# Block-sparse attention and a maxout layer: values as column tiles of TensorE, run in one session with the scores

## The chip, the cores and the metric

The kernel runs on one core of a Trainium2 chip. What counts is the device time of one execution in microseconds, as the median of several runs. A core has five engines that run side by side, each through its own list of instructions in a fixed order: TensorE (PE; its weight loads are shown as PEld), VectorE (DVE), ScalarE (ACT), GpSimd (POOL) and SyncE (SP), which here only issues DMAs. They wait for one another through semaphores. Matmuls write to PSUM, eight banks of 512 f32 per partition; everything else lies in SBUF.

## What is computed

Four batches of eight heads, 768 positions, 64 dimensions a head. A position attends to its neighbours within 15 places and to 24 summaries of blocks of 32 (the maximum of the keys, the mean of the values); the heads' outputs side by side go through a maxout layer.

```
k_sum = k.reshape(B, H, nb, block, D).max(axis=3)
v_sum = v.reshape(B, H, nb, block, D).mean(axis=3)
scores_l = scale * q @ k.T          # masked to |i - j| < 16
scores_s = scale * q @ k_sum.T + log(block)
a = softmax(concatenate([scores_l, scores_s]))
x = a @ concatenate([v, v_sum])     # heads side by side: (3072, 512)
h1 = x @ w1; h2 = x @ w2            # (3072, 1024)
out = maximum(h1, h2) @ w_out       # (3072, 512)
```

## The kernel before

Positions are cut into 12 tiles of 64 queries per head. For a tile, 128 keys stand in the partitions: 64 in its middle, the 32 rows of block summaries (24 used), and 32 of the next tile (`kx`, columns 96 apart). So one matmul per head and tile, with `kx` as weights and 64 queries moving, gives all scores of the tile, keys in the partitions. It contracts over the 64 dimensions of one head. Two heads lie in the two halves of the partitions, so the matmuls of a pair of heads use the upper and the lower 64 rows of the array. Four tiles make a group (`grp` 0 to 2), and a head pair (`hp` 0 to 3) with a group is a *unit*.

`scores` (L473) takes two units in one go: 16 matmuls of 64 rows into two PSUM banks, one bank per head of the pair. In batch 0 the mask is first put into the banks by TensorE (L504: four full matmuls with the identity as weights and `hide`, 0 or -29952, as what moves). In later batches the mask is multiplied in afterwards by VectorE (L545, or twice L549 for the last group, where the window wraps around). Between the two, ScalarE takes the exponential of each bank (L537) into a tile `pb` of four pieces of 192 columns: 64 weights, 64 zeros, 64 weights. The zeros are set once (L246, 12 tiles).

`values` (L558) works on one unit: eight matmuls, each with 128 columns of `pb` as weights and 65 columns of `vx` (values and a one) moving. The zeros let two tiles be accumulated into one output: the first matmul takes weights and zeros, the second zeros and weights, so that one tile's queries come out in partitions 0 to 63 and the other's in 64 to 127. The 65th column is the softmax's denominator: VectorE takes its reciprocal (L580) and multiplies (L582) into `xs`, one unit at a time. `xs` is then turned by TensorE (L594 in batch 0, whole; `turn_x`, L608, in later batches, by half rows) and copied to `xt`.

The maxout layer needs `xt`: `hidden` blocks (L708, eight matmuls of 256 columns with the difference w2 - w1, `wd`), a relu on ScalarE or VectorE (L397, L399), and `out` blocks (L722 on x with w1 w_out, made once by L692; L729 on the relu with w_out), four matmuls of 512 columns each. That is by max(h1, h2) = h1 + relu(h2 - h1).

Every step is recorded by `op` with engine, inputs and outputs (`Plan`, L109); nothing is scheduled when the kernel is built. The string `ORDER` (L20 to L72) lists all 777 steps in one order, with the engine of each (P, A, D, G, S) and the buffer that it takes; per engine, this is the order of the instructions. The costs given to `op` are not used in the run. PSUM's eight banks are one ring that all steps share; so are eight landing buffers `land` for loads. SP's list holds all loads, the stores of the output, and some copies within SBUF that lay out the values (`vx<-vb`, `vx<-vx`).

`first_attention` (L778) does batch 0: k and q are turned whole (L425), scores, then values. `later_attention` (L749) does batches 1 to 3 a head pair at a time: k and q are turned by half rows (`turn_halves`, L440) within the same step as the scores of the pair before (`with_turn`), and a turn of `xs` within another (`with_x`), so that steps which use half the rows stand together. `load_w12` and `split_w12` (L642, L653) load w1 and w2 and make `wd` and `w1b`; `fixed_parts` (L233) makes zeros and masks.

Of the kernel before, what the change touches and what calls it, by code (L numbers as in the profile page):

```python
# [20 lines left out]
    "D11 S23:0,0 D17:0 S27:1 D2 D6 G18 D3 G16:0 D13 S49:2,0 D14 S47:3,0 S48:0 A79:0 G43:0,0,0 G19 P81:0 "  # L21
    "G20 S24:0 G21 A83:2,0 S25:4 D84:0 G28:0,0 D9 S52:5,0 D86 A39 P44:1 G41 S51:0 G88:1 A106:2 S53:6 G42 "
    "A45 P90:2 D89:3 D0 A92:3,0 P91:3 G80:0 A96:0 P108:4 D93:1 G34:0,0 A110:0,0 P82:5 D95 S50:0 D40 A87:1 "
    "D94 D85 D38 S63:7 P97:6,7 D46 S73:1 D26:0 A98:7 D112 A99:2 P35:0 D29 D30 A116:1 P103:1,2 D111:0 "
    "G115:3 S76:3 A36 P118:3 D113 A105:9 D37 S54:0 P117:4 A104:10 G56:0 D123:2 A60:1 P100:5,6 D32 A107:2 "
    "G31 P57:7 S182:4,0 D119:2,0 A102:5 P61:0 D10 P109:2 D120:1 G33 A101:6 P133:1 A114:3 D70:0 P136:3 "
    "S181:0 D121 A58:1,0 P71:4 D137:0 D122 D138:0 P124:6,5 D134:1 D135 D62:0 G74:0 P149:2 A126:2 P152:3 "
    "D150:2 S64:5 D72:0 A125:7 G75:0 D153:0 D151:1 A66:1 P127:7,1 D154 P144:0 G77:0 P141:5 A128:5 P548:4 "
    "D145:1 D142:2 S183:2,0 A129:6 P551:6 A78:0 S184:0 P67:2 P130:3,7 G59:0 D68:0 S185:1,0 P545:1 D146:2 "
    "D143 P157:2 P139:0 P546 G253:0 A140:0 S191:3 A131:2 P549 G22:0 D547:0 A254:1 P147:5 D55:0 P552 "  # L30
    "A132:7 S189:4 P255:0 G65:0 S186:0 A550:0 D553:0 P165:3 P554:7 A256:3,0 D148 S188:0,0 D166:0 D158:1 "
    "P559:4 D167:3 D159:4 A262:3 G261:2 P168:6 D257:0 P176:5 P155:3 G273:0 P555 A156:1 D177:2 D178:5 "
    "P561:2 D8 G198:1,0,0,0 A556:0 D69:0 S187:0 P160:3 P570:5 A562:0 D258 D161:0 A560 D169:1 P557:7 D259 "
    "D162 A260:0 D170 G192:0,0 P173:2 P563:4 D558 P263:3,6,0 A564 S206:6,0 P565:7 D264:0,0 A271:9 S205:0 "
    "P571 D174:2 D265:1 G190:0 S208:2,0 P566 D175 P572 A274:1 D268:1 A269:10 P179:4 P163:6 D196 P567 "
    "A573:0 D164 P199:2 G308:2 A568:1 P171:0 P581:1 D266 A203 D267 A201 D172:2 G309:3 A202 D200 "
    "P275:3,5,6 D270 S204 P575:0 G320:0 S195 D276:2,0 A283:4 S212:5,0 P577:2 A582:1 G197 D576 S207:0 "
    "A281:5 G321:1 P583:5 D277:0 S232:7,0 A280:2 P579:1 D193 A578 S230:3,0 P285:0,3 A580 D180 P588:6 D194 "
    "A288:6 S215:4 P584 A286:2 D282 S209:1,0 D278 P589 D279 D272 D284 P310:7,2,3 S229:0 D287 P293:1 "
    "G359:2 P599:0 D311:0,0 A318:7 G358:3 P302:2 D294:0 P585 A600:2 D295:0 D313 D303:1 P299:1 D304 P597:0 "  # L40
    "A586:2 D289 A315:3 P590 D312:1 A598 P296:2 D319 P593:5 A316:4 D300:2 D314 A591:3 P595:3 D317 A594 "
    "D297:0 G216:0,0 S592 D301:2 P322:4,0,6 D298:1 A596 S210:0 P290:5 S235:0,0 P305:1 A328:5 P601:2 "
    "D291:1 S213:6 D306:2 D292 A330:9 S569 D329 P338:3 A323:3,0 P602 D307 S587 D339:0 D331 S211:0 "
    "P332:4,5,0 A327:0 D340:5 D324:0 G371:0 P347:3 P603 A334:10 D348:1 A336:2 D325 P341:6 D349 P606:7 "
    "D335 A418:1 D337 P350:4 P607 A333:3 D342:2 D351:0 D343:4 D352 P344:3 A604:3 P353:5 D345:1 P608 D326 "
    "D354:2 G214:0 D346:3 D355 P360:6,4,0 A609:1 P356:2 G370:2 A361:0,0 S218:0,0,0 P223:5 D357 G221 "
    "A224:0 A227 G406:3 A225 D362:1 P615:7 A366:6 G246:1,0,0,0 G222 D365:1 A226 P617:2 A368:4 S228 D364 "
    "P613:3 S236:0 D363 A618:0 D5 S605 A616 P372:6,5,0 S220 A614 P611:4 G405:0 D373:2,0 S217 A380:7 "
    "P624:2 A378:5 D612 S219 P619:7 D417:2 S237:2 D374:0 P382:3,5 P625 S239:4 A383:9 D377:2 P620 A385:2 "
    "D375 D376 P631:6 D386 D384 P407:4,3,0 D369 P626 D632:1 A408:0,0 P633:5 A415:10 D627:2 P621 A413:1 "  # L50
    "D367 S628 D410 D381 P629:6 D409:1 A622:3 A634 P390:3 P651:2 D412:3 A630 P635:4 D411 D391:0 D414 "
    "P387:7 D392:0 G238:0,0 P642:5 A636 D15 D388:1 P419:6,0,3 D379 P643 D389:1 A425:4 D416 P637:1 "
    "A420:3,0 D426 P402:7 A427:6 G240:0 P396:6 P644 D397:2 A424:0 D398 P638 D403:0 A652:2 G456:0 D404:2 "
    "S241 A645:2 P399:0 S242 P393:6 D428 P653:3 G244 D400:1 S243 D394:2 D401 S231:0 P649:4 D395 A654 "
    "D421:0 S646 P429:2,7,5 A650 P435:0 G502:3 P639 A433:11 D436:0 D437:3 A431:5 P438:3 D430:0 P647:4 "
    "S234:6,0 P444:7 D432 P660:0 A648 S233:0 D12 D445:1 D439:2 P655:2 D423 S574 D446 D422 P447:5 D440:4 "
    "P661 A640:2 D434 A503:1 D448:0 P247:6 S641 D449 G455:2 P450:4 P441:7 A249 P656 A248 D245 A251 D451:1 "
    "D442:2 D452:5 P662 D443 D250 P453:3 A663:0 P457:1,5,6 D454 P657 G468:0 A458:0,0 P689:0 D467:2 A658:2 "
# [94 lines left out]
def kernel(  # L153
# [14 lines left out]
    nc = tc.nc  # L168
# [673 lines left out]
```

## Time and profile before

| | |
|---|---|
| median of 5 runs | 181.19 us (177.85 to 183.35) |
| profiled execution | 178.53 us |
| its span, first to last instruction | 176.9 us |
| granted TensorE clock | 1.000 |
| moved by DMA | 35.30 MB, mean 200 GB/s |
| instructions on DVE / ACT / POOL | 275 / 155 / 64 |

The page's slices cut the span into 40 parts of 4.4 us; each digit is the busy share in tenths. The groups name a line of the kernel, the engine, the operation, what it writes and reads, and how often; after the bar stand the busy time, the mean length of one in ns, and the idle time just before them with what ended it. In the timeline the first number is the start, the second the length of the merged stretch; matmuls overlap one another in the records (each is shown for some 190 ns or more), so what a stretch costs is read from its start to the start of the next one.

A core's transfers are 25.17 MB read from HBM and 6.29 MB written, and the copies inside SBUF. A load of k or q of a head pair is 384 KB, of half the values of a batch 768 KB, of a half of w1, w2 or w_out 1024 KB.

### The profile page before, as it was taken

The page shows a single profiled execution, that of the slowest core. Times are in us where ns is not written, and L with a number is a line of the kernel's source. Part 1 is how long each engine was busy: PE and PEld are TensorE (multiplying, and loading weights), DVE is VectorE, ACT ScalarE, POOL GpSimd, SP SyncE. Part 2 cuts the span into 40 slices and gives each one's busy share as a digit, 9 for nine tenths or more (in the row PEclk, how much of TensorE's full clock was granted, in tenths as well). Part 3 has the DMA queues.
Part 4 walks back from the last instruction along what each step waited for, and adds up shares of the span by engine and source line. Part 5 has one row for each costly group of instructions (what it writes and reads, how often), then busy time and mean ns, then how long its engine had stood idle before and what let it go on. Part 6 is the DMA issues. An engine that isn't in the chain of part 4 may idle for free.

```text
span 176.9 us, 5119 instructions
## 1 busy us (share of the span) xinstructions
PE 158.2 (89%) x2160; PEld 107.3 (61%) x2160; DVE 109.4 (62%) x275; ACT 95.0 (54%) x155; POOL 50.6 (29%) x64
## 2 busy tenths in 40 slices
PE   0165979999999999979999999799999999999992
PEld 0154756657657676657576675488556657865461
DVE  2219998399879976757978666477565445613030
ACT  3378478576367578849274661585663742140011
POOL 6490545678338413164003751100000000000000
PEclk9999999999999999999999999999999999999999
DMA  5999999999997999977999298555003102100553
GB/s 152 279 308 313 386 386 387 380 366 181 271 367 160 296 280 325 263 224 161 277 213 222 77 208 242 207 153 113 0 4 119 65 0 90 32 0 0 182 175 122
DMA packets 43767, 35.30 MB, mean 200 GB/s; under 512 B 25952, under 2 KB 37728, under 8 KB 43744
## 3 DMA queue, kind: packets, MB, share of 16 engines
q1 hardware_dynamic: 43744, 34.98, 71.5%
q8 instruction: 17, 0.28, 0.7%
q14 instruction: 6, 0.05, 0.1%
HBM read 25.17 MB, written 6.29 MB: 178 GB/s over the span
## 4 chain that ended last, share of the span: by engine, by line
PE 67%; DMA 11%; DVE 7%; SPq 4%; POOL 3%; ACT 3%; issue 3%; POOLq 0%; ACTq 0%
PE banks L708 22%; PE banks L729 19%; PE banks L722 10%; PE banks L569 4%; PE banks L692 4%; DMA out_dram<-o 4%; DMA land<-in_v_dram 4%; DMA land<-in_q_dram 3%; DVE vx L401 3%; PE banks L508 2%; PE banks L440 2%; SPq L296 2%; POOL vb L401 2%; DVE ks L458 2%; ACT o L401 1%
## 5 line engine op out<-in xcount | busy, mean ns | idle before, releaser
L708 PE MATMUL banks<-xt,wd 128*128 128x256 bf16 x384 | 46.2, 273 | 0.5 <-ACT o L401 0.5
L729 PE MATMUL banks<-wo,g 128*128 128x512 bf16 (+1 forms) x200 | 46.6, 371 | 0.0
L708 PEld LDWEIGHTS <-wd 128*128 128x128 bf16 x384 | 36.5, 98 | 7.3 <-issue 0.8
L537 ACT ACTIVATE pb<-banks,bias 128x512 bf16<-128x512 f32 x48 | 31.6, 690 | 15.1 <-PE banks L508 13.6
L397 ACT ACTIVATE g<-banks 128x512 bf16<-128x512 f32 x34 | 20.0, 601 | 22.4 <-PE banks L708 22.4
L729 PEld LDWEIGHTS <-g 128*128 128x128 bf16 x200 | 18.2, 98 | 16.8
L401 POOL CAST kqb<-land 128x768 bf16<-128x768 f32 x20 | 18.4, 920 | 25.6 <-PE banks L440 8.4
L722 PE MATMUL banks<-w1o,xt 128*128 128x512 bf16 (+1 forms) x100 | 24.0, 371 | 0.0
L401 ACT COPY o<-banks 128x512 f32<-128x512 f32 (+1 forms) x19 | 10.6, 567 | 23.9 <-PE banks L729 10.2
L458 DVE TENSOR_REDUCE ks<-kx 128x24 bf16<-128x768 bf16 x16 | 15.2, 947 | 8.1 <-ACT kx L401 8.1
L582 DVE TENSOR_TENSOR xs<-banks,inv 128x256 bf16<-128x256 f32 x48 | 19.1, 415 | 0.5
L401 POOL CAST vb<-land 128x1536 bf16<-128x1536 f32 x7 | 10.4, 1482 | 27.2 <-DMA land<-in_v_dram 25.2
L569 PEld LDWEIGHTS <-pb 128*128 128x128 bf16 x384 | 15.4, 97 | 4.3 <-ACT pb L537 0.2
L580 DVE RECIPROCAL inv<-banks 128x4 f32<-128x4 f32 x48 | 8.2, 177 | 15.9 <-PE banks L569 14.3
L569 PE MATMUL banks<-vx,pb 128*128 128x65 bf16 x384 | 17.5, 193 | 0.1
L722 PEld LDWEIGHTS <-xt 128*128 128x128 bf16 x100 | 9.1, 98 | 8.3
L401 DVE COPY o<-banks 128x512 f32<-128x512 f32 x6 | 4.1, 691 | 15.0 <-PE banks L729 15.0
L399 DVE TENSOR_SCALAR g<-banks 128x512 bf16<-128x512 f32 x14 | 9.7, 690 | 5.6 <-PE banks L708 5.6
L545 DVE TENSOR_TENSOR pb<-pb,mask 128x512 bf16<-128x512 bf16 x24 | 11.5, 485 | 0.9 <-ACT pb L537 0.7
L401 ACT CAST kqb<-land 128x768 bf16<-128x768 f32 x9 | 7.5, 833 | 7.2 <-DMA land<-in_q_dram 5.0
L425 PE MATMUL banks<-identity,kqb 128*128 128x128 bf16 x48 | 5.5, 301 | 5.9 <-ACT kqb L401 5.1
L508 PE MATMUL banks<-qx,kx 64*128 64x64 bf16 (+2 forms) x416 | 10.4, 193 | 0.2 <-ACT qx L401 0.2
(67 smaller groups left out, 170.5 us busy)
## 6 DMA issues: line engine op xcount, KB each, us to landing
land<-in_k_dram SPq DMA_DIRECT2D x16, 384.0 KB, 6.2
land<-in_v_dram SPq DMA_DIRECT2D x8, 768.0 KB, 8.9
land<-in_q_dram SPq DMA_DIRECT2D x16, 384.0 KB, 6.4
out_dram<-o SPq DMA_DIRECT2D x19, 256.0 KB, 3.3
land<-in_moe_w_dram SPq DMA_DIRECT2D x4, 1024.0 KB, 12.3
land<-in_moe_w_out_dram SPq DMA_DIRECT2D x2, 1024.0 KB, 13.7
vx<-vb SPq DMA_DIRECT2D x4, 396.0 KB, 5.2
vx<-vx SPq DMA_DIRECT2D x3, 363.0 KB, 4.3
```

Of the source, the lines that this page charges most:

```text
L397: nc.scalar.activation(out=o, in_=i, func=ACT.Relu)
L399: nc.vector.tensor_scalar_max(out=o, in0=i, scalar1=0.0)
L401: {"DVE": nc.vector.tensor_copy, "ACT": nc.scalar.copy, "POOL": nc.gpsimd.tensor_copy, "SP": nc.sync.dma_start}[e](out=o, in_=i)
L458: op("DVE", 0.95, lambda: nc.vector.tensor_reduce(out=ks.ap[:].rearrange("p (t s) -> p t s", s=2), in_=kt()[:, :, 0:64].rearrange("p t (s ...
L508: nc.tensor.matmul(**m)
L537: op("ACT", 0.7, lambda a=a, pv=pv: nc.scalar.activation(out=pv(), in_=bank(pss[a]).rearrange("p (i w q) -> p i w q", w=2, q=64), func=ACT ...
L545: nc.vector.tensor_tensor(out=pv(), in0=pv(), in1=m, op=ALU.mult)
L569: nc.tensor.matmul(out=av()[:, u, a, :], lhsT=pbs[a].ap[:, 2 * at + u, 64 * par:64 * par + 128], rhs=vx[b].ap[:, 4 * grp + 2 * u + par, 2 ...
L582: op("DVE", 0.42, lambda: nc.vector.tensor_tensor(out=x.ap[:, hp % 2], in0=av()[:, :, :, 0:D], in1=inv.ap[:].to_broadcast([128, 2, 2, D]), ...
L708: nc.tensor.matmul(out=bank(ps)[:, 256 * s:256 * s + 256], lhsT=wd[n].ap[:, c, 128 * s:128 * s + 128], rhs=x_rows(b, grp)[:, c, :], start= ...
L722: nc.tensor.matmul(out=bank(ps, hi - lo), lhsT=x_rows(b, grp)[:, c, sl], rhs=w1o[c].ap[:, lo:hi], start=(c == 0), stop=False)
L729: nc.tensor.matmul(out=bank(ps, hi - lo), lhsT=g.ap[:, f, sl], rhs=wo[f // 2].ap[:, f % 2, lo:hi], start=False, stop=(f == FC - 1))
```

## The change

*Values.* `pb` has no zeros any more: six tiles of two heads by 512 columns. A values matmul takes 64 columns of `pb` as weights instead of 128 and writes 64 partitions, the upper or the lower ones by the parity of the tile. Nothing is accumulated. One step does two units (16 matmuls) into two banks.

*One step, several parts.* The functions `turn_part`, `score_part`, `value_part` and `turn_x_part` give the parts, and `session` puts parts into one TensorE step: a turn, then scores, then values of the units before. In batches 2 and 3 most values go behind the scores of the next units; in batches 0 and 1, and at the end of each batch, they are steps of their own.

*Exp, mask, weighting.* The scores of two units take two neighbouring banks and one exp of 1024 columns; one mask multiplication of 1024; one reciprocal and one multiplication for two units. `xs` is one tile per batch and pair of head pairs.

*Batch 0's mask.* `hide_t`, a transposed mask, is put in by weights of 64 rows, for the two heads in the two halves of the rows, with 512 columns of the identity moving (384 and 128 for the last group). It is made on POOL before the loads arrive; `hide` stays, and `mask` is made from it in two parts.

*Order.* `ORDER` is written anew: 642 steps. SP's list begins k, k, q, q of the first two head pairs, then v; in all of it loads, stores and copies change places. The first `hidden` block stands ahead of the first w1 w_out block on TensorE.

```diff
-    pbr = Ring(tiles("pb", 12, [128, 4, 192], BF16))
+    pbr = Ring(tiles("pb", 6, [128, 2, 512], BF16))
-    xsr = Ring(tiles("xs", 6, [128, 2, 2, 2, D], BF16))
+    xsr = Ring(tiles("xs", 3, [128, NG, 2, 4, D], BF16))
-        for i, t in enumerate(pbr.slots):
-            once(pbr, i, 0.15, lambda t=t: nc.vector.memset(t[:, :, 64:128].bitcast(F32), 0.0), i / 3)
...
+        def make_hide_t():
+
+            nc.gpsimd.memset(hide_t[:], 0.0)
+            nc.gpsimd.memset(hide_t[:, :, 64 + nb:96], NEG)
+            top = hide_t[0:64]
+            keep(top[:, :, 0:64], -1, -1, [[0, 2], [1, 64]])
+            keep(top[:, :, 0:64], 2 * window - 1, 1, [[0, 2], [-1, 64]])
+            keep(top[:, :, 96:128], -2 * window - 1, 1, [[0, 2], [-1, 32]])
+            keep(top[:, 1, 0:64], 47, -1, [[0, 64]])
+            keep(top[:, 1, 96:128], -48, 1, [[0, 32]])
+            nc.gpsimd.tensor_copy(out=hide_t[64:128], in_=top)
...
+    def session(label, prio, parts, us=0.0):
+
+        fns = [part[5] for part in parts]
+        op("PE", us + sum(part[1] for part in parts), lambda: [fn() for fn in fns],
+           read=[r for part in parts for r in part[2]], touch=[r for part in parts for r in part[3]],
+           write=[w for part in parts for w in part[4]], prio=prio,
+           label=" ".join(part[0] for part in parts if part[0]) + label)
+        for part in parts:
+            part[6](prio)
...
+    def score_part(b, units, mask_on, pb):
...
         def head(a):
             r = slice(64 * a, 64 * a + 64)
+            if mask_on == "PE":
+                eye = identity[r, r].rearrange("p (o q) -> p o q", o=1)
+                for i, w in ((slice(0, 3), 0), (slice(3, 4), 1)) if wraps else ((slice(0, 4), 0),):
+                    n = 2 * (i.stop - i.start)
+                    yield dict(out=view(a)[:, :, i], lhsT=hide_t[r, w], rhs=eye.to_broadcast([64, n, 64]),
+                               start=(i.start == 0), stop=False, skip_group_check=True)
...
-            for a in range(2) if mask_on == "PE" else ():
-                for i in range(2):
-                    nc.tensor.matmul(out=view(a)[:, :, i], lhsT=identity[:], rhs=both(hide, i),
-                                     start=(i == 0), stop=False, skip_group_check=True)
...
+        def rest(prio):
+            op("ACT", 1.15, lambda: nc.scalar.activation(
+                out=pb.ap[:].rearrange("p a n -> p (a n)"), in_=bank(ps, 1024), func=ACT.Exp, bias=bias[:], scale=scale),
+               read=[ps], write=[pb], prio=prio, label=f"exp {tag}")
...
+    def value_part(b, units, pb, prio):
...
-            for u in range(2):
-                for a in range(2):
-                    for par in range(2):
-                        nc.tensor.matmul(out=av()[:, u, a, :],
-                                         lhsT=pbs[a].ap[:, 2 * at + u, 64 * par:64 * par + 128],
-                                         rhs=vx[b].ap[:, 4 * grp + 2 * u + par, 2 * hp + a, 0:D + 1],
-                                         start=(par == 0), stop=(par == 1))
+            for c, (hp, grp) in enumerate(units):
+                for u in range(2):
+                    for a in range(2):
+                        for par in range(2):
+                            at = 256 * c + 128 * u + 64 * par
+                            nc.tensor.matmul(out=av()[64 * par:64 * par + 64, c, 2 * u + a, :],
+                                             lhsT=pb.ap[:, a, at:at + 64],
+                                             rhs=vx[b].ap[:, 4 * grp + 2 * u + par, 2 * hp + a, 0:D + 1],
+                                             start=True, stop=True)
...
+                pb = Buf(pbr)
+                parts = [score_part(b, units, "DVE", pb)]
+                if units[0][0] == hp and after:
+                    parts.insert(0, start_turn(*after))
+                if hp == 3 and units[0][0] != hp:
+                    parts.insert(0, turn_x_part(b, 0))
+                if waiting:
+                    parts.append(value_part(b, *waiting, prio + 10))
+                session("", prio + 5, parts, 0.28 if waiting else 0.19)
+                waiting = units, pb
+                if b == 1 and parts[0][0] != "turn x10 ":
+                    session("", prio + 10, [value_part(b, *waiting, prio + 10)], 0.19)
+                    waiting = None
```

## The prediction

> **What bounds the kernel now.** I read the page's busy shares and slices first, then TensorE's waits, then its timeline in the dense part to price one session of each kind, then the groups of the touched lines.
>
> ```profile
> span 176.9 us, 5119 instructions
> PE 158.2 (89%) x2160; PEld 107.3 (61%) x2160; DVE 109.4 (62%) x275; ACT 95.0 (54%) x155; POOL 50.6 (29%) x64
> PE   0165979999999999979999999799999999999992
> DVE  2219998399879976757978666477565445613030
> DMA  5999999999997999977999298555003102100553
> ...
> PE banks L665 <- DVE w1b L401: 1.6, 1, 1.6
> PE banks L337 <- POOL vb L401: 1.2, 1, 1.2
> ...
> PE banks L440 <- DVE vx L401: 0.7, 1, 0.7
> PE banks L708 <- ACT o L401: 0.5, 1, 0.5
> ```
>
> After 27 us TensorE is never idle but for the last three waits, 2.4 us together; before that it has little to do, and VectorE and the transfers fill the slices. So the end is: when the dense part begins, plus TensorE's own work, plus 2.4 us, plus a tail of 3.2 us (173.7 to 176.9). The work is priced from starts in the timeline:
>
> ```profile
> 78.35 0.52 PE L337 MATMUL banks<-vb,amean 128*32 128x128 bf16 x24 [1.25 <-POOL vb L401]
> 78.80 2.79 PE L708 MATMUL banks<-xt,wd 128*128 128x256 bf16 x24
> 81.52 0.52 PE L440 MATMUL banks<-identity,kqb 64*128 64x64 bf16 x24
> 81.88 0.40 PE L508 MATMUL banks<-qx,kx 64*128 64x64 bf16 x16
> 82.21 1.05 PE L708 MATMUL banks<-xt,wd 128*128 128x256 bf16 x8
> ...
> 28.21 0.66 PE L569 MATMUL banks<-vx,pb 128*128 128x65 bf16 x16
> 28.70 0.60 PE L504 MATMUL banks<-hide,identity 128*128 128x256 bf16 x4
> 29.24 0.41 PE L508 MATMUL banks<-qx,kx 64*128 64x64 bf16 x16
> ```
>
> Eight full matmuls of 256 columns take 0.87 us (rows of L708 one behind another), so the 24 from 78.80 are through at 81.41; the half-row session begins at 81.52: 0.11 us to change the array's shape. Its 24 transposes take 0.36, its 16 scores 0.22, and 0.11 us to change back ends at 82.21. Sixteen values matmuls (two heads' units) take 28.70 - 28.21 = 0.49 us, 30.6 ns each, with no change of shape. With these prices, and 0.863 us per four 512-column matmuls, the program's TensorE list adds to 152.2 us. Start time minus the sum of the list up to there is 19.1 us at the first later turn (start 37.5), 20.1 after the wait at 78, 21.4 from 121 on: the ledger closes to 0.1 us, and any work taken off TensorE is worth its full time unless something else is then late.
>
> ```profile
> L569 PE MATMUL banks<-vx,pb 128*128 128x65 bf16 x384 | 17.5, 193 | 0.1
> L537 ACT ACTIVATE pb<-banks,bias 128x512 bf16<-128x512 f32 x48 | 31.6, 690 | 15.1 <-PE banks L508 13.6 <-DVE pb L246 1.1
> L545 DVE TENSOR_TENSOR pb<-pb,mask 128x512 bf16<-128x512 bf16 x24 | 11.5, 485 | 0.9 <-ACT pb L537 0.7
> L582 DVE TENSOR_TENSOR xs<-banks,inv 128x256 bf16<-128x256 f32 x48 | 19.1, 415 | 0.5
> ```
>
> **The change, part by part.**
>
> *Values as column tiles.* The number of matmuls stays, 16 for two units, but each has 64 weight columns and a twin in the other half of the array. No row before has 64-column tiles. Nearest are L508, twin tiles of half the rows (16 in 0.22 us), and L337, four column tiles of 32 (24 matmuls of 128 columns in 0.45 - 0.11 = 0.34 us, 14 ns each, a quarter of a full one of 128). Both say that tiles overlap: 16 in 0.235 us. Against it speaks the Trainium skill, TensorEngine Tiling (Array Packing), Restrictions: column tiling switches Fast Weight Load off; TensorE: Matmul & The Clock Gate, section LDWEIGHTS, has an unaided load at columns / 1.2 ns, 53 ns for 64. Then each twin waits for its weights and 16 take 0.43 us. L337 cannot decide: 32 columns, 27 ns by that formula, hide behind 53 ns of matmul. No twin at all would be about 0.47. I take 0.235, as the nearest row that has two tiles and short matmuls; 0.22 (L508's pace) and 0.47 are the ends.
>
> Of 24 pairs, 14 stay alone: 0.11 + 0.235 + 0.11 = 0.455 against 0.49, -0.5 us together. Ten ride behind scores: one more change of shape, 0.11 + 0.235 = 0.345 against 0.49, -1.45 us. The change from half rows straight to half columns is in no row; 0.11 is what every other one costs, nothing and 0.22 (by way of the full shape) are its ends, 1.1 us either way. Sum -1.95; at 0.43 it is +2.7, at 0.47 +3.7.
>
> *First batch's mask by row halves.* Before, mask and scores of a session took 28.70 to 29.24, 0.54, and the scores with the change back 0.34 (27.87 to 28.21). After, 512 columns by two half-row tiles at once: 0.216 (half of 0.43) + 0.222 + two changes = 0.66. Six sessions: -1.3 us. TensorE's list is then 148.9 us, -3.25.
>
> *Exp, mask, weighting for two.* ACT's copies of 256 and 512 elements (372 and 590 ns) give 0.85 ns an element, so one exp of 1024 is 1.12 us for two of 0.69: 24 x (1.12 - 1.38) = -6 us of ACT. Masks: single ones of 512 and 256 mostly took 417 and 284 ns, so 1024 take 0.68, and 18 of them 12.3 us for the 17 that L545 and L549 have. Reciprocals halve (-4 us), weighting goes from 0.415 twice to 0.69 (the 512-column PSUM copies on VectorE), -3.4, and 12 zeroings of 165 ns go. VectorE loses some 14 us. I price all this at nothing in the dense part: TensorE hides it. What gets longer is the chain from scores to values: 1.12 + 0.68 = 1.8 against 1.26 + 0.42 = 1.7 us, and the order puts at least two full TensorE blocks (1.73 us) and mostly more between; where it does not, 0.1 to 0.3 us a pair, 2 us over a batch or two at worst. Score banks are now held as a pair until the long exp ends: same cover.
>
> *Setup on POOL.* The new half-row mask is five selects of 0.29, two memsets and a copy, about 2.2 us, behind the old one (done at 4.2). POOL then was idle until 7.8, and the first scores come after 11: hidden; uncovered it is 2.2 us at the start. The multiplied mask goes from 1.27 to about 2.5 us in POOL's queue, behind two of the subtractions L655 and ahead of batch 1's casts, whose turns are 6 us away.
>
> *The new order.* SP now asks for both first heads' k and q, then v, and for all of q and k of batch 0 before the weights. I chained VectorE's list by hand with the durations of its rows: first k placed at 5.9 us, sums done at 11.4 (first scores 12 against 15.4), v spread at 18, values at about 19 instead of 24.7. But then the list runs without a gap: maxima, w1b, spread of v's second half, xt. The pieces needed by the first hidden block (L708) are ready at about 32 us, when TensorE's list is at 12.4: an offset of 19.5. The next blocks wait for wd 3 on POOL (32.3) and wd 2 on VectorE (34.9), which makes it about 20.1 against 19.1: +1.0 us. I hold this to +-1.5, since the landing of the weights is read from other neighbours in the queue.
>
> *Waits in the dense part.* v of batch 2 was asked for when 22.5 MB had gone before, and TensorE waited 1.25 us for its cast; now about 20.0 MB. At the old pace it lands near 68, is cast by 71 and is needed at 54.3 + 20.1 = 74.4: that wait goes. Next late would be k of batch 2: needed at 63.6 instead of 67.3, with 17.3 MB ahead of it, landing near 61 with a cast of 0.9: just in time. I put -1.0 us for all waits (1.4 left).
>
> **Sum:** -3.25 + 1.0 - 1.0 = -3.2 us: span 173.7, execution 178.53 - 3.2 = 175.3. The median of the five runs shown, 181.19, lies 2.7 us above the profiled one, so on the median's footing it is 178.0. Between the two, nearer the median, I forecast 177.5.
>
> **The rivals.**
> 1. *Weights set the pace of the column tiles.* List 153.6 to 154.6 us, other terms as above: +1.4 to +2.5, about 182.5 on the median's footing. For it: the skill's rule; against it: L337's tiles. Chance 0.14.
> 2. *The transfers decide (slower).* TensorE's fixed order asks for batch 2 about four us earlier, but the DMA row is at nine tenths up to 90 us, and SP issues in order. Place: the turn of k of batch 2 and the means behind it. It decides as soon as all waits grow by more than 2.25 us over before's 2.4 (3.25 less the 1.0 lost at the start), which k landing at 65 instead of 61 does. With 6 us more of waits: +3.75, 184.9 on the median's footing. For it: the longest wait before came from a load. Against: the loads were moved up with their use. Chance 0.18.
> 3. *More than the sum.* The start gives 1 us rather than costs it and all waits go: -3.25 - 1 - 2.4 = -6.6, 174.5. Chance 0.10.
>
> **How the numbers follow.** The forecast case has 0.58; its own range, from the +-1.5 of the start, about as much of waits and the footing, is 174 to 181. The whole range reaches into rivals 1 to 3: 172.5 to 184.5. About 2% is what a measurement of this kernel can tell from no change, 3.6 us of 181. Faster: 0.39 from the forecast case and 0.10 from rival 3, 0.49. Within 2%: 0.15 + 0.06 (rival 1) + 0.04 (rival 2) = 0.25. Slower: 0.04 + 0.08 + 0.14 = 0.26.
>
> **What would show it.** Sixteen values matmuls starting within 0.24 us, twins some 3 ns apart, show the tiles right; 0.43 or more shows rival 1. The first L708 block at 31 to 34 us shows the start right. Waits of TensorE after 35 us under 2.5 us in all show the transfers kept up; 5 or more, at a turn of k or the means, is rival 2. The list's 148.9 us is wrong if start time minus list grows where no wait stands. The forecast fails if the mixed session costs more than 0.11 us for its middle change.

## The result, and the profile after

| | before | after |
|---|---|---|
| median of all runs | 181.08 us (73 runs, 177.85 to 184.58) | 179.22 us (38 runs, 177.29 to 183.34) |
| after / before | | 0.997, 95% interval 0.9945 to 0.9994 |
| profiled execution | 178.53 us | 182.13 us |
| its span | 176.9 us | 180.4 us |

The ratio, and every median called undisturbed below, leaves out on both sides the runs that lie more than 1.5% above the fastest of their kernel. The undisturbed medians are 179.36 us before and 178.62 after; the medians of all runs stand at 0.990. In a second group of runs the same kernel after came to 179.15 us against 181.86, ratio 0.9895 (0.9852 to 0.9939), undisturbed 178.09 against 179.74. So the change is worth between a third of a per cent and one per cent, and no difference of 2% is seen. The forecast was 177.5 us, a gain of 3.7. By the medians of all runs 1.9 of it came, by the undisturbed ones 0.7, and 1.7 in the second group.

The two profiled executions lie on opposite sides of their medians. The profile after is therefore read for *where* its time lies, with its own span as the sum, and not for the difference between the kernels.

First the page of the kernel after: span, busy times, then the rows of slices.

```profile
span 180.4 us, 5008 instructions
PE 159.1 (88%) x2152; PEld 103.3 (57%) x2152; DVE 106.7 (59%) x197; ACT 91.4 (51%) x121; POOL 48.4 (27%) x71
...
PE   0379739999999929999999999999999999999992
...
PEclk9999997999999995899999999999999999999999
DMA  5999999999999996999999789491001104201133
```

Before, PE's row was a wall of nines from 27 us on, with two 7s and the last slice. Now there is a 2 in the slice from 63 to 68 us, and in the clock's row, in the slice behind it (68 to 72), a 5. DMA is at nine tenths up to 99 us, but for a 6 in that same slice. The same page's groups for the lines that the prediction priced:

```profile
L571 PE MATMUL banks<-vx,pb 128*64 128x65 bf16 x384 | 11.5, 204 | 3.8 <-DMA vx<-vx 3.7
...
L529 ACT ACTIVATE pb<-banks,bias 128x1024 bf16<-128x1024 f32 x24 | 26.7, 1115 | 29.0 <-PE banks L526 27.1
...
L539 DVE TENSOR_TENSOR pb<-pb,mask 128x1024 bf16<-128x1024 bf16 x18 | 13.2, 736 | 1.2 <-ACT pb L529 1.2
L580 DVE TENSOR_TENSOR xs<-banks,inv 128x512 bf16<-128x512 f32 x24 | 16.6, 690 | 0.6
```

Exp 1115 ns, mask 736, weighting 690: priced at 1.12 us, 0.68 and 0.69. The values matmuls are busy for 11.5 us against 17.5. What is new stands at the end of the first row: 3.8 us of idle time before them, 3.7 of it for a DMA. The list of TensorE's waits has the same item:

```profile
...
PE banks L664 <- POOL w1b L407: 4.2, 1, 4.2
PE banks L571 <- DMA vx<-vx: 3.7, 1, 3.7
...
PE banks L707 <- POOL wd L654: 0.2, 1, 0.2
```

The first is at 21 to 26 us, before the dense part. The second is the 2 in PE's row. `vx<-vx` is the copy inside SBUF that spreads the key means of batch 1 over `vx`; the values of batch 1 need it. TensorE's timeline there (start, length, what):

```profile
64.05 0.22 PE L571 MATMUL banks<-vx,pb 128*64 128x65 bf16 x1
67.97 0.65 PE L571 MATMUL banks<-vx,pb 128*64 128x65 bf16 x15 [3.71 <-DMA vx<-vx]
68.56 0.82 PE L446 MATMUL banks<-identity,kqb 64*128 64x64 bf16 x24
69.19 0.62 PE L526 MATMUL banks<-qx,kx 64*128 64x64 bf16 x16
69.74 1.89 PE L707 MATMUL banks<-xt,wd 128*128 128x256 bf16 x8
71.55 0.65 PE L571 MATMUL banks<-vx,pb 128*64 128x65 bf16 x16
```

The wait is 3.7 us, and it is not all. The 24 transposes from 68.56 take 0.63 us to the scores instead of the 0.36 of before, and the eight matmuls of 256 columns from 69.74 take 1.81 to the next session; at full clock they are 0.87 and a change of shape of 0.11. The windows say why (stretch; busy times and counts of PE, PEld, DVE, ACT, POOL; granted clock; DMA share; GB/s):

```profile
66.00:68.00 2.00, 0.03 (x2) 0.03 (x2) 0.00 (x0) 0.00 (x0) 0.00 (x0) 0.78 0.74 139
68.00:70.00 2.00, 2.00 (x57) 1.78 (x58) 1.24 (x3) 0.15 (x1) 0.82 (x1) 0.50 0.25 55
70.00:72.00 2.00, 2.00 (x24) 1.28 (x22) 0.27 (x1) 1.99 (x3) 0.53 (x1) 0.50 0.98 221
72.00:74.00 2.00, 2.00 (x13) 0.80 (x10) 1.72 (x3) 0.95 (x2) 1.71 (x2) 0.51 0.96 174
74.00:76.00 2.00, 2.00 (x25) 0.94 (x23) 0.97 (x4) 0.00 (x0) 0.69 (x1) 1.00 0.85 226
```

In the pause all engines stand still; for some six us behind it the clock is granted at half. The queue shows when the copy was asked for (SP's own timeline, then the chain that ended last, both of the kernel after):

```profile
55.44 0.60 SPq L407 DMA_DIRECT2D vx<-vx  x1
56.09 0.60 SPq L302 DMA_DIRECT2D land<-in_q_dram  x1
56.73 12.71 SPq L324 DMA_DIRECT2D land<-in_v_dram  x2
```

```profile
55.44 12.50 DMA vx<-vx
67.97 0.65 PE banks L571 x15
```

SP issued it at 55.44, nine us ahead of its use, and it landed 12.5 us later: with the earlier loads in front of it and a q and two v loads issued right behind it. The three copies of this kind in the page land after a median of 5.1 us.

Now the ledger of the prediction, start time of TensorE minus the sum of its list up to there, worked out from the starts in each trace:

| TensorE's list at | before | after |
|---|---|---|
| first later turn | 19.1 (at 37.5 us) | 21.0 (at 41.0 us) |
| ahead of the late values | | 21.0 (59.8) |
| behind them | | 25.1 (68.6) |
| near 78 us | 20.1 | 27.3 |
| at the end | 21.4 | 28.0 |
| list, tail | 152.2, 3.2 | 148.95, 3.4 |

The offset stays level wherever no wait and no lowered clock stands, so the list's prices hold to some tenths of a us. The sum of after is 148.95 + 28.0 + 3.4 = 180.4 us. Against the sum forecast, 173.7, the start is 0.9 us worse than said, and in this execution the dense part loses 7.0 us where 1.4 were left for it: 3.7 of wait with 0.4 around it, 2.3 behind it at half clock, 0.7 later.

### The profile page after: what moved, and what is told of

The parts are those of the page before. It is cut to its first block, busy times and chain, and to the rows that moved or that the text cites. A ratio compares the mean times of both kernels' runs of the same rounds, so it can differ in the third digit from the quotient of the medians.

```text
span 180.4 us, 5008 instructions
## 1 busy us (share of the span) xinstructions
PE 159.1 (88%) x2152; PEld 103.3 (57%) x2152; DVE 106.7 (59%) x197; ACT 91.4 (51%) x121; POOL 48.4 (27%) x71
## 4 chain that ended last, share of the span: by engine, by line
PE 63%; DMA 21%; SPq 8%; DVE 3%; POOL 2%; issue 1%; POOLq 0%; DVEq 0%
PE banks L728 21%; PE banks L707 19%; PE banks L721 10%; SPq L302 7%; DMA vx<-vx 7%; DMA land<-in_v_dram 5%; DMA land<-in_moe_w_dram 5%; PE banks L571 4%; DMA land<-in_k_dram 4%; PE banks L526 3%; PE banks L446 2%; PE banks L620 2%; PE banks L664 1%; DVE wd L654 1%; DVE xt L407 1%
## 5 line engine op out<-in xcount | busy, mean ns | idle before, releaser
L529 ACT ACTIVATE pb<-banks,bias 128x1024 bf16<-128x1024 f32 x24 | 26.7, 1115 | 29.0 <-PE banks L526 27.1
L407 POOL CAST kqb<-land 128x768 bf16<-128x768 f32 x25 | 20.6, 839 | 46.1 <-DMA land<-in_k_dram 27.9
L403 ACT ACTIVATE g<-banks 128x512 bf16<-128x512 f32 x32 | 19.1, 599 | 15.0 <-PE banks L707 14.8
L407 ACT COPY o<-banks 128x512 f32<-128x512 f32 (+1 forms) x14 | 8.0, 572 | 24.4 <-PE banks L728 23.6
L407 DVE COPY o<-banks 128x512 f32<-128x512 f32 (+1 forms) x11 | 7.2, 665 | 17.3 <-PE banks L728 14.4
L580 DVE TENSOR_TENSOR xs<-banks,inv 128x512 bf16<-128x512 f32 x24 | 16.6, 690 | 0.6
L407 DVE COPY kx<-banks 128x768 bf16<-128x768 bf16 x10 | 9.5, 951 | 12.2 <-PE banks L446 7.4
L577 DVE RECIPROCAL inv<-banks 128x8 f32<-128x8 f32 x24 | 4.9, 205 | 19.9 <-PE banks L571 19.8
L571 PE MATMUL banks<-vx,pb 128*64 128x65 bf16 x384 | 11.5, 204 | 3.8 <-DMA vx<-vx 3.7
L539 DVE TENSOR_TENSOR pb<-pb,mask 128x1024 bf16<-128x1024 bf16 x18 | 13.2, 736 | 1.2 <-ACT pb L529 1.2
L571 PEld LDWEIGHTS <-pb 128*64 128x64 bf16 x384 | 8.6, 115 | 8.1 <-DMA vx<-vx 3.8
L407 ACT COPY qx<-banks 128x768 bf16<-128x768 bf16 x15 | 12.0, 800 | 2.0 <-DVE kx L407 1.8
```

What stands on the lines that cost most here:

```text
L403: nc.scalar.activation(out=o, in_=i, func=ACT.Relu)
L407: {"DVE": nc.vector.tensor_copy, "ACT": nc.scalar.copy, "POOL": nc.gpsimd.tensor_copy, "SP": nc.sync.dma_start}[e](out=o, in_=i)
L529: op("ACT", 1.15, lambda: nc.scalar.activation(out=pb.ap[:].rearrange("p a n -> p (a n)"), in_=bank(ps, 1024), func=ACT.Exp, bias=bias[:], ...
L539: nc.vector.tensor_tensor(out=o, in0=o, in1=m, op=ALU.mult)
L571: nc.tensor.matmul(out=av()[64 * par:64 * par + 64, c, 2 * u + a, :], lhsT=pb.ap[:, a, at:at + 64], rhs=vx[b].ap[:, 4 * grp + 2 * u + par, ...
L580: op("DVE", 0.7, lambda: nc.vector.tensor_tensor(out=x.ap[:, grp] if g1 == grp else x.ap[:, grp:g1 + 1, hp % 2], in0=av()[:, :, :, 0:D], i ...
```

## The experiments

Each kernel was run in five rounds against the kernel before. Its median is that of all runs (undisturbed ones are named), the ratio is to the kernel before of the same group (medians 181.86 us in the first, 181.47 in the second, 181.29 in the third). In `ORDER` the first letter of a step is its engine (S the DMA queue, D VectorE, P TensorE), the number the step.

### First group: which term failed

**The kernel after, once more.**

> The changed kernel once more, as the baseline of this group. If the wait of TensorE for the spread of batch 1's means (3.7 us in the first profile, followed by some 6 us at half the granted clock) belongs to the kernel and not to that one execution, the same wait at L571 stands here again, at 62 to 68 us, longer or shorter; if it was an accident, the ledger's offset stays at 21 past 70 us.

179.15 us (177.19 to 185.02), 0.9895. Its profiled execution has a span of 180.3 us, almost the same, and loses it in another place. TensorE and then VectorE near 91 us:

```profile
90.90 0.44 PE L571 MATMUL banks<-vx,pb 128*64 128x65 bf16 x15 [1.17 <-DMA vx<-vx]
93.05 5.32 PE L707 MATMUL banks<-xt,wd 128*128 128x256 bf16 x32 [1.70 <-DVE o L407]
```

```profile
91.83 0.56 DVE L407 CAST kqb<-land 128x768 bf16<-128x768 f32 x1 [3.96 <-DMA land<-in_k_dram]
92.31 1.28 DVE L407 COPY o<-banks 128x512 f32<-128x512 f32 x2
```

The spread of batch 1 was 1.2 us late here, that of batch 2 another 1.2. Then the last k of batch 2, issued at 82.73, kept VectorE waiting for 4.0 us to 91.8. Behind its cast in VectorE's list stand the copies that free TensorE's banks, so TensorE waited 1.7 us for `o`. Its 32 matmuls of 256 took 5.3 us; they take 3.5 at full clock. The offset went from 20.8 to 28.1, of it 4.9 between 89 and 102 us. The sum is the same, the late item another: what is common is that a transfer was late and that the clock fell behind the wait.

**Batch 1's means spread by VectorE**, not by the queue:

```diff
-... P442:1 G163 G272:3 S169 D243:1 P252:6 ...
+... P442:1 G163 G272:3 D169 D243:1 P252:6 ...
```

> The copy that spreads batch 1's block means goes from SP's queue to VectorE, at the same place of the order; nothing else moves. Theory (its landing behind loads is what TensorE waits for): the wait at L571 and the half clock behind it vanish, start time minus list stays near 21 past 70 us, the profile's span is 174 to 175.5 us, and the time is 1 to 2.5% below the changed kernel's. Rival (the loads of batch 2 are late as well, and the next of them takes its place): a wait of 2 us or more at the turn of batch 2's k or at its means, and under 0.5% of gain.

177.84 us (175.31 to 179.7), 0.9803 (0.9758 to 0.9848): 1.3 us under the kernel after in the same group, 0.9 by the undisturbed medians (177.18 against 178.09). Its waits of TensorE:

```profile
PE banks L526 <- DVE kx L471: 1.0, 1, 1.0
PE banks L707 <- DVE o L407: 1.0, 1, 1.0
...
PE banks L571 <- DVE xs L580: 0.4, 1, 0.4
PE banks L446 <- ACT qx L407: 0.3, 1, 0.3
PE banks L707 <- DVE xt L407: 0.3, 1, 0.3
```

No wait for `vx<-vx` is left and the clock is not lowered after 35 us; the span is 175.5 us, the offset 23.2 at the end. So having this copy in the queue does cost, some 1 us in the median against some 6 in the profile of after: that execution had it at its worst. Two things change with the move, and this run does not part them: TensorE needs no landing any more, and SP, which stood for 1.3 us until the source of the copy was there, asks for v of batch 2 at 53.6 us instead of 56.7. About 3 us of other waits remain. The first two rows look like the price of the move: VectorE's own spread takes 3.2 us (54.1 to 57.3), and TensorE waits for `o` and `kx`, which stand behind it in VectorE's list, at 63 and 66 us.

**Batch 0's mask by full matmuls again**, four of 256 columns with `hide` and the identity, in place of the half-row ones:

```diff
+            for a in range(2) if mask_on == "PE" else ():
+                for i in range(2):
+                    nc.tensor.matmul(out=view(a)[:, :, 2 * i:2 * i + 2], lhsT=identity[:], rhs=both(i),
+                                     start=(i == 0), stop=False, skip_group_check=True)
```

> Batch 0's mask is put in by four full matmuls of 256 columns, as before the change, in place of the two half-row ones of 512. Theory (the six sessions lie before TensorE is the bound): TensorE's list grows by 1.3 us but the time by at most 0.3 us, with the first L707 block where it was. Rival (TensorE's work counts everywhere, as my sum had it): +1.3 us, 0.7%.

178.92 us (176.26 to 182.16), 0.9902 (0.9851 to 0.9953), the same as the kernel after. The 1.3 us of list that the half-row mask saves are worth nothing. They lie before 32 us, where TensorE waits for w1, `wd` and casts, and what the list loses the start's offset gains: the first later turn comes at 41.2 us here, and at 40.7 to 41.2 in three profiles with the mask by row halves (after, after once more, and the next run).

**Column tiles without a twin beside them**: all eight matmuls of the even tiles, then all of the odd ones.

```diff
-                for u in range(2):
-                    for a in range(2):
-                        for par in range(2):
+                for par in range(2):
+                    for u in range(2):
+                        for a in range(2):
```

> The values matmuls go in another order: all of the upper column tile of two units, then all of the lower, so that no twin stands beside another. Theory (twins overlap, and a load of 64 columns hides behind a matmul of 65): 16 take 0.47 us instead of 0.235, and with 18 such sets in the dense part the time grows by 4.3 us, 2.4%. Rival[...]: 16 take 0.85 us or more and the time grows by 11 us. Rival (pairing gives nothing): no change.

179.45 us (177.43 to 182.63), 0.993 (0.9878 to 0.9982), not to be told from the kernel after. Sixteen matmuls start within 0.275 us in its trace, within 0.247 in that of after. In both they start as two chains some tens of ns or less apart, though here the program gives one half of the columns after the other; how the second half gets ahead the run does not show. So the order of the twins matters little, and a weight load of 64 columns does not set the pace. By the rule weighed in the prediction (the Trainium skill, TensorE: Matmul & The Clock Gate, LDWEIGHTS: columns / 1.2 ns, which makes an estimate of 53 ns for 64) sixteen would take 0.43 us in two chains and 0.85 in one; the trace disagrees with both.

As the time is the same, its profiled execution, 179.08 us, also shows the kernel after nearer to its median than the two others do. The clock is not lowered after 35 us, and TensorE's waits there, but for pauses of under 0.2 us, are:

```profile
PE banks L707 <- DVE o L407: 1.6, 1, 1.6
...
PE banks L707 <- ACT o L407: 1.1, 1, 1.1
...
PE banks L571 <- DMA vx<-vx: 0.2, 1, 0.2
```

The spread of batch 1 is in time here. ScalarE's `o` at 78 us waits for a store to land, VectorE's at 90 us stands behind the cast of the late k, as in the second profile of after. So this execution loses less than the two profiles of after, and none of it by the spread of batch 1.

### Second group: are the transfers it?

**All later batches' means spread by VectorE** (`S169`, `S193`, `S217` to D).

> The changed kernel with the spreads of the block means of all three later batches on VectorE instead of SP's queue, at their places in the order. Theory (each such copy lands behind loads, and batch 2's is late too: 1.2 us at the values of batch 2 in one profile): no wait for a copy within SBUF is left at the values, all waits of TensorE after 35 us under 2.5 us, the time 0.3 to 1% below that of the run with batch 1's means alone moved. Rival (VectorE's list is now too long around 80 to 90 us): another wait at a mask, a reciprocal or a copy out, no further gain.

184.2 us (182.52 to 185.9), 1.0296 (1.0112 to 1.0481). The waits changed sides:

```profile
PE banks L707 <- DVE o L407: 3.9, 3, 2.2
...
PE banks L728 <- DVE g L405: 1.4, 1, 1.4
```

What VectorE does for the means it does later for `o` and `g`: one spread moved gains, three lose.

**The same three in the kernel before** (there `S204`, `S228`, `S252`).

> The kernel before, with the same three spreads on VectorE. Theory (before, TensorE reached these places later and after them in the queue's order, and its profile has no wait for such a copy): within 0.5% of before. Rival (the spreads in SP's queue cost every order as much, so that moving them is a gain of its own that has nothing to do with the change): 1% or more faster than before.

188.95 us (186.19 to 190.65), 1.047 (1.0249 to 1.0691), with 4.6 us of waits for `kx` and 2.0 for `g`, both VectorE's. It is VectorE's list again, and the kernel before had 3 us more of it (109.4 us busy against 106.7). This run does not say what one spread alone would do in before.

**Light loads**: of q, k and v of batches 2 and 3 an eighth is loaded, with the same number of DMAs and the same work behind them.

```diff
-                out=view(), in_=src[b, 2 * hp:2 * hp + 2].rearrange("h (p j) d -> p h (j d)", j=J)),
+                out=view()[:, :, 0:384 if b < 2 else 48],
+                in_=src[b, 2 * hp:2 * hp + 2].rearrange("h (p j) d -> p h (j d)", j=J)[:, :, 0:384 if b < 2 else 48]),
...
-                out=view().rearrange("p h m d -> p (h m) d"),
-                in_=v[b, 4 * n:4 * n + 4].rearrange("h (m r) d -> r (h m) d", r=128)),
+                out=view().rearrange("p h m d -> p (h m) d")[:, 0:24 if b < 2 else 3],
+                in_=v[b, 4 * n:4 * n + 4].rearrange("h (m r) d -> r (h m) d", r=128)[:, 0:24 if b < 2 else 3]),
```

> The changed kernel with the loads of q, k and v of batches 2 and 3 cut to an eighth of their bytes (48 of 384 columns, 3 of 24 pieces; the rest of the landing buffers keeps what earlier loads left, so these batches come out of other numbers). Same instructions on all engines. Theory (the transfers decide in the dense part): waits after 35 us fall under 1.5 us, no half clock after 35 us, start time minus list 21 to 22.5 to the end, span 173 to 175.5, 2 to 3% below the changed kernel. Rival (waits come from the order of ScalarE's and VectorE's lists): 3 us of waits or more remain and the time moves by less than 1%.

175.05 us (174.28 to 175.51), 0.9781 (0.9689 to 0.9873). Its six runs lie within 1.2 us; the six of any other kernel that was run so often lie within 2.5 to 5.1. In its waits of TensorE one line is left after 35 us (the lines' numbers are one higher here):

```profile
PE banks L665 <- POOL w1b L408: 4.0, 1, 4.0
...
PE banks L572 <- DVE vx L408: 0.2, 1, 0.2
```

The place where after stood still for 3.7 us now reads:

```profile
63.67 0.44 PE L572 MATMUL banks<-vx,pb 128*64 128x65 bf16 x16
64.05 0.52 PE L447 MATMUL banks<-identity,kqb 64*128 64x64 bf16 x24
```

The offset is 20.6 at 41 us and 20.7 at 124: the span of 173.1 is 148.95 + 20.7 + 3.4. Row by row it rises by 0.2 at that wait and by 0.3 at 77 to 81 us (32 matmuls of 256 columns take 3.8 us to the next row instead of 3.5), so the list is right to about half a us over these 83 us. The prediction's list and its ledger hold where the data is there, and nearly all of the loss of the dense part goes with these loads.

**The same light loads in the kernel before.**

> The kernel before with the same loads cut. Theory: its 2.4 us of waits shrink to about 1, 1% faster; the light changed kernel is then faster than it by what TensorE's list lost less what the start lost, 3.25 - 1.9 = 1.3 us, 0.7%. Rival (the change has no gain even where nothing is late): the two light kernels within 0.3% of each other.

179.69 us (175.94 to 180.85), 0.9893 (0.9839 to 0.9946). The medians of the two light kernels lie 4.6 us apart, but the undisturbed ones (177.32 and 175.05) 2.3, and the ratios 1.1%. The theory had 1.3 us. So without late loads the change is worth some 2 us, with them 0.7 to 1.7. The profiled execution of this kernel, 180.85 us, is none of the undisturbed ones: its dense part began 2.5 us later than in before's, behind waits for `vx` and `w1b` of VectorE (1.2 and 2.0 us) and with a clock of 0.73 from 25 to 31 us, where the profile of before has 1.00. So the start of the kernel before is not fixed either, and the cut loads come only behind it.

### Third group: the late k, and the start

**k of batch 2's last head pair asked for earlier**, right behind its q:

```diff
-... S177:3,0 D283:1,0 ... S193 P476:5 A483 S176:0 A296:1,0 ...
+... S177:3,0 S176:0 D283:1,0 ... S193 P476:5 A483 A296:1,0 ...
```

> The changed kernel with one load moved: k of batch 2's last head pair is asked for right behind q of the same pair, ahead of three loads of k for batch 3, a store and two copies. Nothing else moves. Theory (its cast stands in VectorE's list ahead of the copy out that frees the bank TensorE needs at 91 us, and the load lands too late): the 1.7 us wait of L707 for a copy out there is gone, the offset does not jump by more than 1.5 us between the turns of k 22 and k 23, time 0.3 to 1% below the changed kernel. Rival (those who were moved back are late instead, batch 3's k): the same loss at a turn of batch 3 after 105 us.

177.63 us (176.26 to 181.34), 0.9877 (0.9772 to 0.9982). The wait for VectorE's `o` is gone from the profile. Between 88 and 98 us the offset still grows by 1.5, now for the spread of batch 2's means, which TensorE waits for by 1.2 us; and at 78 us it waits 1.6 us for ScalarE's `o`, whose buffer waits for a store to land. Partly right: k was one of the late items, and the others are close by. The median is 1.5 us under that of the kernel after in the other groups, the ratio hardly differs from its 0.9895.

**Both, k early and batch 1's means on VectorE.**

> The same move of one load, and batch 1's spread of the means on VectorE as well. Theory (the two waits are separate, each from one place in SP's list): the gains add; 1.2 to 2% below the changed kernel, waits after 35 us under 2.5 us, span 174 to 175.5. Rival (the transfers as a whole bound the dense part, and a wait that is removed comes back): no faster than with the spread alone moved.

177.58 us (176.48 to 181.21), 0.9892 (0.9814 to 0.997). It is no faster than either alone. No wait is left near 91 us, but those behind VectorE's own spread are back: 1.1 us for `o` at 64 us and 0.8 for `kx` at 67.

**The first scores ahead of the first w1 turn**, on top of both:

```diff
-... D98 D99 P46:5 A30 D49:1 P110:0 D27 ...
+... D98 D99 A30 D49:1 P110:0 P46:5 D27 ...
```

> As the one before, and on TensorE the first turn of w1 stands behind the first scores of head pairs 2 and 3, which need nothing of w1. Theory (these scores wait only because they stand behind it): scores at 24 instead of 26 us, the first L707 block earlier by 0.5 us or more, 0.3% faster. Rival (the landing of w2's first half and the subtraction on POOL set the first L707 block, at 31.7 us at the earliest): within 0.2% of the one before.

177.25 us (175.82 to 178.87), 0.9862 (0.9753 to 0.997), the lowest median and profiled span (174.1 us) of those that compute all. The scores start at 23.5 us instead of 26.7 in the kernel with both, and the first hidden block at 31.65 instead of 32.29. The second unit's block then waits for `wd` of POOL (33.68), and the time gained, 0.3 us of median, is within the scatter.

**TensorE kept busy before the first w1 turn** by 36 transposes of the identity, on top of both:

```diff
+            for _ in range(36 if n == 0 else 0):
+                nc.tensor.transpose(out=bank(ps, 1024, BF16)[:, 0:128], in_=identity[:], identity=identity[:])
```

> As the second of this group, and 36 transposes of the identity stand ahead of the first turn of w1, in its bank, where TensorE is idle for 4 us; they add work and change no result. Theory (idle time makes the clock drop, and the work after it runs at half speed): granted clock 0.95 or more from 25 to 31 us where it was 0.78, TensorE's work there done sooner, and the first L707 block up to 0.8 us earlier. Rival: the clock holds but the first L707 block stays within 0.3 us, as it waits for w2's first half; or the clock drops all the same.

177.37 us (176.21 to 178.72), 0.9896 (0.9797 to 0.9994). The window of 25 to 31 us of this kernel, then of the one without the transposes:

```profile
25.00:31.00 6.00, 4.47 (x108) 3.54 (x110) 5.13 (x8) 3.81 (x5) 3.94 (x3) 1.00 1.05 387
```

```profile
25.00:31.00 6.00, 5.18 (x102) 4.15 (x103) 4.74 (x8) 3.96 (x6) 2.91 (x3) 0.72 1.05 388
```

The clock holds at 1.00 instead of 0.72, and TensorE is busy for less time with about the same work. The first hidden block comes at 31.98, 0.3 us earlier than the 32.29 of the kernel without them, about what the rival allowed, and the time does not follow by more than the scatter. Part of what the clock saves is waited away again: 0.9 us ahead of the block, mostly for VectorE's `xs`, where the kernel without the transposes has 0.5, and 0.7 instead of 0.4 for `wd` behind it. The start is held by data more than by TensorE's clock.

## Why the prediction failed

The time forecast lay 1.7 us off the median, within its range; the gain was forecast at twice the one of the medians, and at five times that of the undisturbed ones. Two terms of the sum failed: the start, put at +1.0 us, measured +1.9, and the waits, put at -1.0, measured +0.3 in the first comparison and -0.6 in the second (undisturbed medians, with the starts as profiled). To see that, take from a time what lies around the span (1.6 us before, 1.7 after), the list and the tail. What is left is the offset at the end: the start and all waits and lowered clocks of that execution. It is worked out so for runs without a profile too:

| offset at the end, us | before | after | difference |
|---|---|---|---|
| lowest run (177.85, 177.29) | 20.9 | 23.2 | +2.4 |
| undisturbed medians (179.36, 178.62) | 22.4 | 24.6 | +2.2 |
| the same of the second group (179.74, 178.09) | 22.7 | 24.0 | +1.3 |
| medians of all runs (181.08, 179.22) | 24.1 | 25.2 | +1.1 |
| the same of the second group (181.86, 179.15) | 24.9 | 25.1 | +0.2 |
| profiled (178.53, 182.13) | 21.4 | 28.0 | +6.6 |
| light loads, undisturbed medians (177.32, 175.05) | 20.3 | 21.0 | +0.7 |

The prediction had +1.0 for the start and -1.0 for the waits: 0.0. By its steps:

- **Values as column tiles: right.** 0.247 us for sixteen against 0.235 taken and 0.43 by the rule of weight loads. From one set to the next block it is 0.38 us where 0.345 was said, less than 1 us over the 24 sets. The middle change of shape, from half rows straight to half columns, is no dearer than others: in the light kernel, scores start at 86.89 and values at 87.22, 0.33 us for 0.22 of scores and 0.11. Rival 1 is out.
- **TensorE's list, 148.9 us: right.** The offset is level to half a us over 83 us of the light kernel, whose span of 173.1 lies 0.6 from the sum's 173.7.
- **Exp, mask, weighting, POOL's setup: right, hidden.** Only the mask took longer than priced, 0.74 us for 0.68. In the light kernel TensorE's waits after 35 us are 0.2 us together, so no chain from scores to values shows.
- **The start, +1.0: mis-sized, it measured +1.9** (21.0 against 19.1 in the profiles). The first hidden block came at 32.6 us where offset and list (19.5 + 12.4) put it at 31.9, and 0.8 went behind it where 0.6 were said. The sum let the block start when its data is there. In the trace the block itself waits for none: TensorE starts on w1 at 25.6 us, after 4.2 us of waiting for its cast, and has only one gap of 0.4 us from there to the block. What was missing is TensorE's own pace in this stretch, where the granted clock is 0.72. How much of the 0.7 us is the clock's stays open: held at 1.00 it brought the block forward by 0.3 us, and the scores moved ahead by 0.6, with the next wait for data close behind in both. With the mask's row halves the start is one account: 1.3 us off the list, 1.9 on the offset, 0.6 lost together where 0.3 were to be gained. That the time follows such a mend could not be shown: it moved by 0.2 to 0.3 us, inside the scatter.
- **The waits, -1.0 with 1.4 left: wrong, they shrank by less or not at all.** They were read from one execution of before, which was near its lowest run. With the starts as profiled, the table leaves for the waits +0.3 and -0.6 in the undisturbed medians, +0.5 in the lowest runs, -0.8 and -1.7 in the medians of all, +4.7 in the profiles. An undisturbed execution of after loses some 3 to 3.6 us in the dense part (24.0 and 24.6, less 21.0). The shrunk loads show that it is the transfers', for with them 0.4 is left of it (21.0 less the 20.6 at its start). In before the same cut takes some 2.2 us off the undisturbed median (179.53 in that group to 177.32), in after 3.0 to 3.6. So the kernel before had most of this loss as well, the forecast had it in the 2.7 us between before's profile and its median without naming it, and with the change it is some 1 us larger.
- **Which wait: half named.** Rival 2 said k of batch 2 and the means behind it. The first late item was the copy that spreads batch 1's means, which the working had looked at only for when it is issued, nine us ahead; that it may take 12.5 us to land, and that SP stands for 1.3 us ahead of it, was not counted. Put on VectorE it gave back 1.3 us of median, 0.9 undisturbed. The late k of batch 2 came second, with stores that free `o` beside it; moving k as well gave nothing on top that could be measured. The prediction's sign for rival 2, waits of 5 us or more after 35 us, is met in one of the two profiles of after (5.1 us; 3.7 in the other). Its six us were what the profiled execution shows, and more than the median has.
- **The clock behind a wait: missing.** 3.7 us of idle cost 2.3 more at half clock, so that wait was worth 1.6 times its length.
- **The last choice.** The sum gave 178.0 on the median's footing; 177.5 was taken between two footings, with nothing in the sum for it.

By the undisturbed medians the shortfall of the first comparison is then 3.0 us = 3.7 - 0.7: 0.9 of the start, 0.5 of the last choice, 0.3 of a longer tail and of what lies around the span, and 1.3 of the waits. In the second comparison it is 2.1, with the same first three and 0.4 of the waits. By the medians of all runs it is 1.8 and 1.0, with waits that shrank by about as much as said, or by 0.7 more. This split rests on starts seen in two profiles. They are not fixed: other profiled executions of the two kernels and of edits that leave the start alone have 20.2 to 21.2 after and 18.9 and 21.5 before. A later start in the median execution of before would shift weight from the start to the waits, and that stays open, as does whether the copy's 12.5 us come from the backlog ahead of it or from the v loads behind it.

Among the versions that compute all, the spread of batch 1 by VectorE has the best ratio (0.9803), and the one with k and the first scores moved as well the lowest median (177.25 us). Their intervals overlap, and those of the second reach to the change alone; by medians both are 1 to 2 us better than it.

## What to carry to other kernels

Count work taken off the bounding engine only where that engine is what all others wait for: here two fifths of it (1.3 of 3.25 us) lay ahead of the dense part and were worth nothing. When an engine gets ahead, list for each queue what it will ask for next, copies inside SBUF among it, with time of issue, landing under load and need; and price a wait of some microseconds with the lowered clock behind it. A single profile near the lowest run hides the waits of the typical one: look where it stands among the runs first, and to see whether transfers make the difference, shrink the loads and keep everything else.

## What the runs showed of the hardware

- **The clock behind a pause.** 3.7 us of idle brought 0.50 for about six us; two waits of 1.2 and 1.7 us close together also stretched 32 matmuls from 3.5 to 5.3 us, at 0.50. One wait of 1.6 us at the same place (the unpaired tiles) did not: 3.6 us. Ahead of w1's turn, 3.1 us of idle were followed by 0.53 from 25 to 27 us; with transposes in the pause 2.5 us of idle were left, and the clock stayed at 1.00.
- **Column tiles.** 64-column tiles with 65 columns moving run at 15.4 ns each (0.247 us / 16), half of a full one's 30.6, and 17 ns when the two halves are not given in turns.
- **A copy inside SBUF.** 363 KB landed 12.5 us after issue in one case; the median of the three such copies was 5.1 us in that execution, 8.8 in the other one of the same kernel, and 4.4 with light loads.
- **Busy queues that carry less.** At a DMA share above one, the stretch of 56 to 64 us moved 187 GB/s in the kernel after and 281 in the kernel before:

```profile
56.00:64.00 8.00, 8.00 (x94) 4.99 (x88) 6.22 (x11) 6.71 (x10) 0.89 (x2) 1.00 1.13 187
```

```profile
56.00:64.00 8.00, 8.00 (x124) 5.28 (x123) 7.75 (x20) 4.34 (x9) 4.08 (x5) 1.00 1.01 281
```

  The share alone would have called both full. Why it carries less was not tried.
- **Where the same program waits.** Two profiled executions of the kernel after, 182.13 and 182.05 us, lost most of it at 64 us in one and at 91 us in the other.
